# A decode block on one core: the first half of the output rows moves to partitions 28 to 31, and one store replaces two

## The chip, the core and the metric

The kernel runs on one core of a Trainium2 chip. The core has TensorE (PE; its loads of stationary operands are shown apart, as PEld), VectorE (DVE), ScalarE (ACT), GpSimd (POOL) and SyncE (SP), and 16 DMA engines that SP's and ACT's queues feed. The metric is the device time in microseconds (us) of one execution; the median of several runs is compared.

## The reference

One token for each of two sequences (B = 2, D = 448) goes through a normalization, an attention over the last W = 2048 positions of a cache of 8192, and a gate:

```python
xn = layernorm(x)
q = (xn @ wq)                       # 16 heads of 256; 8 KV heads
p = softmax(q . k[:, :, -2048:] * 256 ** -0.5)
s = (p @ v[:, :, -2048:]) @ wo      # back to 448
g = silu(relu(xn @ w1) @ w2)        # 448 -> 1792 -> 448
return x + s * g                    # (2, 1, 448), bfloat16
```

All inputs are bfloat16. The kernel reads 44 MB and writes 1792 bytes.

## The kernel before

The work is split into NU = 4 units: a unit is one sequence and four KV heads, with a K block and a V block of 4 MB each. `_Prog` collects the operations of each engine in a list; each engine runs its list in order, and a list entry names the operations that it waits for (its `deps`), which become waits on semaphores. `pr.dma(SP, ...)` puts a transfer in SP's list, `pr.dma(ACTE, ...)` in ACT's. Nearly all transfers are in SP's list, in this order: wq, w1, w2, the four K blocks, the V blocks (each into its K block's place, once the scores of that unit are done), then wo in five pieces (`WO_PARTS`: 20, 4, 5, 2 and 1 of 32 slices). The lists of PE and DVE are cut at marks into blocks with branches between them (`emit_pe`, `emit_dve`), which bring their code in ahead of time; the order of the work stays as written.

The order of the stages: normalization and clearing of the banks; q = xn @ wq; the gate (`do_H`, `do_F`); for each unit the transposes of K on DVE (L361), the scores (`do_S`), the maximum and the exponential (`do_max`), the transposed weights (`do_et`); then `do_spread` and `do_pt`, the products with V (`do_PV`, `do_out`) and the turning of the result into `at2`, 32 slices of 2 columns each (`do_turn_out`). The matmul instructions all carry the line of the helper `mm`, L313.

The output is kept as four groups of 112 columns (NCOL), numbered c = 2k + h. Group c of sequence b lies in partition 32h + 2b + k: the two groups with h = 0 in partitions 0 to 3, those with h = 1 in partitions 32 to 35. ROWS = 36 partitions are worked on together, those between without use. A row gets to its partition by the stationary operand of the matmul that makes it: two columns of data stand among zero columns in a row of PADW = 5, and a window of 4 columns that starts one column earlier or later (`1 - k : 5 - k`) moves the data to row 2b or 2b + 1. This is done in four places:

- `m_xc` brings x into this layout (stationary `xpad`); ACT copies it to `x_c`, in two copies (L334), POOL has cleared `x_c` before (L251).
- the end of `do_F` does it for the gate (`fpad`, L480), where ACT and DVE then make `g_sb`.
- the tail: `do_turn_out` has filled `at2`. The first 24 slices of wo are multiplied with 2-column stationaries into `wbk` in four column groups of the array (L538), DVE copies `wbk` to `wc` (L541), and four matmuls with `fpad` (float32; each is two records, so 8) bring the sum into `fbk` in the layout above (L547).
- the last 8 slices of wo are multiplied with windows of `at2` straight into the same rows of `fbk` (L553): 8 slices by 4 groups, 32 matmuls, which wait for the third, fourth and fifth piece of wo.

Then DVE multiplies `fbk` with the gate (L559), adds `x_c` (L561) and the two halves leave by two stores, one issued by SP and one by ACT (L563); SP waits for both (L564):

```python
d_o = [pr.dma(eng, half(out, h), out_sb[32 * h:32 * h + 4, :], [v_o]) for h, eng in ((0, SP), (1, ACTE))]
pr.op(SP, None, d_o)
```

Of the kernel before, what the change touches and what calls it, by code (L numbers as in the profile page):

```python
# [5 lines left out]
BF = mybir.dt.bfloat16  # L6
F32 = mybir.dt.float32
ACT = mybir.ActivationFunctionType
ALU = mybir.AluOpType
AX = mybir.AxisListType  # L10

PE, DVE, ACTE, SP, POOL = "pe", "dve", "act", "sp", "pool"
# [121 lines left out]
def bass_recurrent_scan__sliding_block_cached__dense_activation_relu__decode_kernel(  # L134
# [11 lines left out]
    B, Sq, D = A_x.shape  # L146
# [14 lines left out]
    NCOL = D // 4  # L161
    ROWS = 36
    QC = 448
    XW = 160
    PADW = 5
    WO_PARTS = [20, 4, 5, 2, 1]
    WO_TILED = 24

    es = contextlib.ExitStack()
    with es:  # L170
        pr = _Prog(nc, es)

        def named(name, shape, dt):
            return es.enter_context(nc.sbuf_tensor(name, shape, dt))
# [4 lines left out]
        def view(t, off, dims, n=128, p0=0):  # L179
            width = t.shape[1]  # L180
            return bass.AP(t, p0 * width + off, [[width, n]] + dims)
# [6 lines left out]
        wqo = named("wqo", [128, 32 * D], BF)  # L188
# [3 lines left out]
        ident = named("ident", [128, 128], BF)  # L192
# [6 lines left out]
        f8 = named("f8", [128, 8], F32)  # L199
        asel = named("asel", [128, 72], BF)  # L200
        x_sb = named("x_sb", [128, D], BF)
        x_c = named("x_c", [128, NCOL], BF)
# [10 lines left out]
        h_sb = named("h_sb", [128, 448], BF)  # L213
        zc = named("zc", [128, D], F32)
        wc = named("wc", [128, D], F32)
        fpad = named("fpad", [128, PADW], F32)
        xpad = named("xpad", [128, PADW], BF)
        ea = named("ea", [128, NCOL], F32)
        g_sb = named("g_sb", [128, NCOL], F32)
        tmp = named("tmp", [128, NCOL], F32)  # L220
        out_sb = named("out_sb", [128, NCOL], BF)
# [8 lines left out]
        rs = named("rs", [128, 2 * NU], F32)  # L230
        pt = [named(f"pt{i}", [128, 512], BF) for i in range(NU)]
        o_odd = named("o_odd", [128, DH], F32)
        at2 = named("at2", [128, 32 * PADW], BF)

        sbk = [psum(f"sbk{i}", [128, 512], F32) for i in range(2)]
        obk = psum("obk", [128, 512], F32)
        spk = psum("spk", [128, 512], F32)
        mbk = psum("mbk", [128, 512], F32)
        qbk = psum("qbk", [128, 512], F32)
        wbk = psum("wbk", [128, 512], F32)  # L240
        fbk = psum("fbk", [128, 512], F32)

        def half(t, h):
            return t.rearrange("b s (k h n) -> h (b s k) n", h=2, n=NCOL)[h]

        def kv_src(u, cache):
            b, hg = divmod(u, 2)
            return cache[b, 4 * hg:4 * hg + 4, SK - W:SK, :].rearrange("g (p t) d -> p g (t d)", t=NT)

        d_x = pr.dma(ACTE, x_sb[0:B, :], A_x[:, 0, :])  # L250
        p_xc = pr.op(POOL, lambda e: e.memset(x_c[:, :], 0.0))  # L251
        wq_src = A_wq.rearrange("r (hf c) -> (r hf) c", hf=2).rearrange("(p s) c -> p (s c)", s=SLOTS)
        w1_src = B_w1.rearrange("r (hf c) -> (r hf) c", hf=2).rearrange("(p s) c -> p (s c)", s=SLOTS)
        w2_src = B_w2.rearrange("(p j) n -> p (j n)", j=14)
# [3 lines left out]
        st = {}  # L258
# [3 lines left out]
        for u in range(NU):  # L262
# [4 lines left out]
            out=ident[:, :], in_=ident[:, :], compare_op=ALU.not_equal, fill=1.0,  # L267
            base=0, pattern=[[-1, 128]], channel_multiplier=1), [i0])
        p_z = [pr.op(POOL, lambda e, t=t: e.memset(t[:, :], 0.0))
               for t in (fpad, xpad, asel, rm, bt, qstat, at2)][-1]  # L270
# [4 lines left out]
            out=sd[0:B, 0:1], in0=st2[0:B, 1:2], scalar1=EPS, scalar2=None, op0=ALU.add), [v_ag])  # L275
# [5 lines left out]
        def z(t):  # L281
            return a_z[t.name]
# [10 lines left out]
        v_pm = pr.op(DVE, red(pmask[:, :], view(ident, 0, [[1, 4], [4, 32]])))  # L293
        v_g8 = pr.op(DVE, red(view(g8, 0, [[2, 4], [1, 2]]), view(ident, 0, [[32, 4], [1, 2], [2, 4]])))
        v_f8 = pr.op(DVE, red(f8[:, :], view(ident, 0, [[1, 8], [8, 16]])))
        v_fp = pr.op(DVE, lambda e: e.tensor_copy(view(fpad, 1, [[2, B]]), f8[:, 0:B]), [v_f8, p_z])
        v_xp = pr.op(DVE, lambda e: e.tensor_copy(view(xpad, 1, [[2, B]], n=B), ident[0:B, 0:B]), [p_z])
        v_h2 = pr.op(DVE, red(half2[:, :], view(ident, 0, [[8, 2], [16, 8], [1, 8]]), AX.XY))
        v_gs = pr.op(DVE, lambda e: e.tensor_copy(
            view(gsum, 0, [[8, 16], [1, 8]]), view(g8, 0, [[0, 16], [1, 8]])), [v_g8])  # L300
# [11 lines left out]
        def mm(out_ap, lhsT, rhs, start, stop=False, **kw):  # L312
            return lambda e: e.matmul(out_ap, lhsT=lhsT, rhs=rhs, start=start, stop=stop,  # L313
                                      skip_group_check=True, **kw)
# [13 lines left out]
        deps = [v_xp, d_x, z(sbk[1])]  # L328
        for c in range(4):
            k, h = divmod(c, 2)  # L330
            m_xc = pr.op(PE, mm(sbk[1][32 * h:32 * h + 4, 0:NCOL], xpad[0:B, 1 - k:5 - k],
                                x_sb[0:B, NCOL * c:NCOL * c + NCOL], k == 0, k == 1, tile_position=(0, 32 * h)), deps)
            deps = []
        d_xc = [pr.op(ACTE, lambda e, h=h: e.activation(  # L334
            x_c[32 * h:32 * h + 4, :], sbk[1][32 * h:32 * h + 4, 0:NCOL], ACT.Copy), [m_xc, p_xc]) for h in range(2)]

        deps = [d_wq, v_xr, z(qbk)]
        for s in range(SLOTS):
# [24 lines left out]

        def do_S(u):
            b, hg = divmod(u, 2)
            deps = [st["turn", u], st["q"], z(sbk[u % 2]), d_xc[1], st.get(("exp", u - 2))]
            for jp in range(8):
                j, par = divmod(jp, 2)
                for g in range(4):
                    o = pr.op(PE, mm(sbk[u % 2][32 * g:32 * g + 8, :],  # L370
                                     view(qstat, jp * 16 + 4 * g + 2 * hg + b, [[128, 8]]),
                                     view(kv[u], 64 * j + 2 * g + par, [[DH, NT], [8, 8]]),
                                     jp == 0, jp == 7, tile_position=(0, 32 * g)), deps)
                    deps = []
            last_S[u] = o
# [70 lines left out]
        def do_turn_out(hg):  # L446
            deps = [st["osb", 2 + hg], v_as, st["mbk"]]
            lo = 64 * hg
            for dq in range(8):
                o = pr.op(PE, mm(mbk[lo:lo + 64, 288:352], asel[:, 7 - dq:71 - dq],  # L450
                                 view(o_sb, hg * 2 * DH + 32 * dq, [[DH, B], [1, 32]]),
                                 dq == 0, dq == 7, tile_position=(0, lo)), deps)
                deps = []
            st["at"] = st["mbk"] = pr.op(DVE, lambda e: e.tensor_copy(
                view(at2, 1, [[2, B], [PADW, 32]], n=64, p0=lo), view(mbk, 288, [[32, B], [1, 32]], n=64, p0=lo)), [o, p_z])

        def do_H():
            deps = [st["w1"], v_xh, v_q]
# [10 lines left out]
        def do_F():  # L469
            deps = [st["w2"], st["h"], z(fbk)]  # L470
            for j in range(14):
                i = j % 4
                o = pr.op(PE, mm(fbk[32 * i:32 * i + B, 0:D], h_sb[:, 32 * j:32 * j + 2], w2_sb[:, j * D:j * D + D],
                                 j < 4, j >= 10, tile_position=(0, 32 * i)), deps)
                deps = []
            v = pr.op(DVE, lambda e: e.tensor_copy(zc[:, :], fbk[:, 0:D]), [o])
            deps = [v, v_fp, st["mbk"]]
            for c in range(4):
                k, h = divmod(c, 2)
                o = pr.op(PE, mm(mbk[32 * h:32 * h + 4, 0:NCOL], fpad[:, 1 - k:5 - k],  # L480
                                 zc[:, NCOL * c:NCOL * c + NCOL], k == 0, k == 1, tile_position=(0, 32 * h)), deps)
                deps = []
            a_e = pr.op(ACTE, lambda e: e.activation(ea[0:ROWS, :], mbk[0:ROWS, 0:NCOL], ACT.Exp, scale=-1.0), [o])
            v = pr.op(DVE, lambda e: e.tensor_scalar(
                out=ea[0:ROWS, :], in0=ea[0:ROWS, :], scalar1=1.0, scalar2=None, op0=ALU.add), [a_e])
            v = pr.op(DVE, lambda e: e.reciprocal(tmp[0:ROWS, :], ea[0:ROWS, :]), [v])
            st["g"] = st["mbk"] = pr.op(DVE, lambda e: e.tensor_tensor(
                out=g_sb[0:ROWS, :], in0=mbk[0:ROWS, 0:NCOL], in1=tmp[0:ROWS, :], op=ALU.mult), [v])
# [46 lines left out]
        deps = [st["at"], z(wbk)]  # L535
        for j in range(WO_TILED):
            i = j % 4
            o = pr.op(PE, mm(wbk[32 * i:32 * i + B, 0:D], view(at2, PADW * j + 1, [[2, B]]), wqo[:, j * D:j * D + D],  # L538
                             j < 4, j >= WO_TILED - 4, tile_position=(0, 32 * i)), deps + [landed.get(j)])
            deps = []  # L540
        v_wc = pr.op(DVE, lambda e: e.tensor_copy(wc[:, :], wbk[:, 0:D]), [o])  # L541
# [2 lines left out]

        for c in range(4):
            k, h = divmod(c, 2)
            pr.op(PE, mm(fbk[32 * h:32 * h + 4, 0:NCOL], fpad[:, 1 - k:5 - k],  # L547
                         wc[:, NCOL * c:NCOL * c + NCOL], k == 0, tile_position=(0, 32 * h)), deps + [v_wc])
        for j in range(WO_TILED, 32):
            for c in range(4):  # L550
                k, h = divmod(c, 2)
                lo = j * D + c * NCOL
                m_o = pr.op(PE, mm(fbk[32 * h:32 * h + 4, 0:NCOL], at2[:, PADW * j + 1 - k:PADW * j + 5 - k],  # L553
                                   wqo[:, lo:lo + NCOL], False, j == 31,
                                   tile_position=(0, 32 * h)), deps + [landed.get(j)])
                deps = []
# [2 lines left out]
        v_t = pr.op(DVE, lambda e: e.tensor_tensor(  # L559
            out=tmp[0:ROWS, :], in0=fbk[0:ROWS, 0:NCOL], in1=g_sb[0:ROWS, :], op=ALU.mult), [m_o, st["g"]])  # L560
        v_o = pr.op(DVE, lambda e: e.tensor_tensor(  # L561
            out=out_sb[0:ROWS, :], in0=tmp[0:ROWS, :], in1=x_c[0:ROWS, :], op=ALU.add), [v_t] + d_xc)
        d_o = [pr.dma(eng, half(out, h), out_sb[32 * h:32 * h + 4, :], [v_o]) for h, eng in ((0, SP), (1, ACTE))]  # L563
        pr.op(SP, None, d_o)  # L564
        pr.op(PE, None, [v_o])

        pr.run()
# [28 lines left out]
```

## Time and profile before

| | |
|---|---|
| median of 3 runs | 110.27 us (109.98 to 110.44) |
| profiled execution, its own time | 110.19 us |
| its span, first to last instruction | 108.9 us |
| mean granted TensorE clock | 0.859 |
| PE / DVE / ACT / POOL busy | 60.8 / 62.3 / 9.5 / 2.2 us |
| DMA | 44.16 MB, mean 406 GB/s |

The span is that of one profiled execution; the time of an execution is longer by what lies around it (1.3 us here). The profile is a page of the whole span and views that a trace answers. In the page's slices each digit is the busy share of 1/40 of the span in tenths. In a group's row, `out<-in (partitions x elements, type) xcount` is followed by the busy time, the mean ns of one and the idle time of the engine before it with what ended it. In the chain of waits each line is start, length, engine, what was worked on. Rows of an issue (`DMA_DIRECT2D`, engine with a q) last as long as the engine's sequencer was busy with issuing, not as long as the transfer. Matmul ends are modelled.

### The profile page before, as it was taken

The page shows a single profiled execution, that of the slowest core. Times are in us where ns is not written, and L with a number is a line of the kernel's source. Part 1 is how long each engine was busy: PE and PEld are TensorE (multiplying, and loading weights), DVE is VectorE, ACT ScalarE, POOL GpSimd, SP SyncE. Part 2 cuts the span into 40 slices and gives each one's busy share as a digit, 9 for nine tenths or more (in the row PEclk, how much of TensorE's full clock was granted, in tenths as well). Part 3 has the DMA queues.
Part 4 walks back from the last instruction along what each step waited for, and adds up shares of the span by engine and source line. Part 5 has one row for each costly group of instructions (what it writes and reads, how often), then busy time and mean ns, then how long its engine had stood idle before and what let it go on. Part 6 is the DMA issues. An engine that isn't in the chain of part 4 may idle for free.

```text
span 108.9 us, 1103 instructions
## 1 busy us (share of the span) xinstructions
PE 60.8 (56%) x459; PEld 16.4 (15%) x459; DVE 62.3 (57%) x87; ACT 9.5 (9%) x20; POOL 2.2 (2%) x14
## 2 busy tenths in 40 slices
PE   0002195943000069929961996299538966769672
PEld 0001023411000001101100220012023222303131
DVE  1933007344299979999999999940448332203021
ACT  4735000000000000002000200020020000000000
POOL 7000000000000000000000000000000000000000
PEclk9999999999655557995998599769965699999999
DMA  6899999999999999999999999999999899999960
GB/s 165 337 438 405 413 433 493 411 433 470 433 397 433 470 433 397 433 470 433 397 409 494 433 397 409 494 433 397 409 494 433 373 409 439 427 417 428 385 245 1
DMA packets 2471, 44.16 MB, mean 406 GB/s; under 512 B 290, under 2 KB 548, under 8 KB 804
## 3 DMA queue, kind: packets, MB, share of 16 engines
q1 hardware_dynamic: 2456, 44.11, 95.1%
q8 instruction: 3, 0.05, 0.2%
q10 hardware_dynamic: 12, 0.00, 0.0%
HBM read 44.11 MB, written 0.00 MB: 405 GB/s over the span
## 4 chain that ended last, share of the span: by engine, by line
DMA 55%; DVE 29%; PE 9%; SPq 4%; issue 1%
DMA kv<-in_A_k_cache_dram 33%; DVE kv L361 24%; DMA wqo<-in_A_wo_dram 22%; PE sbk L313 7%; SPq L39 4%; PE fbk L313 1%; PE wbk L313 1%; DVE q_x L390 1%; DVE rm L378 1%; DVE wc L541 1%; DVE rm_t L380 0%; DVE bias L384 0%; DVE bt L381 0%; DVE tmp L559 0%; DVE out_sb L561 0%
## 5 line engine op out<-in xcount | busy, mean ns | idle before, releaser
L313 PE MATMUL sbk<-kv,qstat 128*8 128x512 bf16 x128 | 30.0, 1091 | 21.3 <-DVE kv L361 21.3
L361 DVE STREAM_TRANSPOSE kv<-kv 128x2048 f32<-128x2048 f32 x16 | 35.6, 2275 | 3.0 <-DMA kv<-in_A_k_cache_dram 3.0
L313 PEld LDWEIGHTS sbk<-kv,qstat 128*8 128x8 bf16 x128 | 4.9, 107 | 44.9 <-DVE kv L361 27.2
L313 PE MATMUL obk<-kv,pt 128*16 128x512 bf16 x128 | 9.5, 441 | 2.5 <-DVE xg L442 1.2
L439 DVE TENSOR_SCALAR o_odd<-obk,rs 128x256 f32<-128x256 f32 x4 | 1.9, 484 | 11.1 <-PE obk L313 11.1
L385 ACT ACTIVATE e_sb<-sbk,bias 128x512 bf16<-128x512 f32 x4 | 2.7, 687 | 50.2 <-DVE bias L384 50.2
L313 PE MATMUL sbk<-kv,f 128*8 128x512 f32 x14 | 7.0, 620 | 0.0
L378 DVE TENSOR_REDUCE rm<-sbk 128x1 f32<-128x512 f32 x4 | 2.6, 662 | 4.8 <-PE sbk L313 4.8
L313 PE MATMUL qbk<-wqo,xr 128*4 128x512 bf16 x28 | 3.2, 626 | 3.9 <-DMA wqo<-in_A_wq_dram 3.9
L313 PE MATMUL mbk<-ident,xg 2*128 2x2 bf16 x7 | 0.3, 160 | 8.6 <-issue 8.6
L313 PEld LDWEIGHTS obk<-kv,pt 128*16 128x16 bf16 x128 | 3.2, 97 | 8.7 <-issue 5.0
L313 PE MATMUL qbk<-w_sb,xg 128*128 128x448 bf16 x14 | 4.4, 495 | 0.0
L344 DVE TENSOR_SCALAR q_x<-qbk 128x512 bf16<-128x512 f32 x1 | 0.7, 691 | 6.3 <-PE qbk L313 6.3
L390 DVE STREAM_TRANSPOSE q_x<-e_sb 128x512 bf16<-128x512 bf16 x4 | 2.8, 691 | 1.7 <-ACT e_sb L385 1.7
L407 DVE TENSOR_TENSOR pt<-spk,pmask 128x512 bf16<-128x512 f32 x4 | 2.6, 684 | 0.7 <-PE spk L313 0.7
L541 DVE COPY wc<-wbk 128x448 f32<-128x448 f32 x1 | 0.6, 624 | 3.8 <-PE wbk L313 3.8
L313 PE MATMUL spk<-q_x,perm 128*32 128x128 bf16 x16 | 0.6, 294 | 3.1 <-DVE q_x L390 3.1
L355 DVE CAST qstat<-mbk 32x256 bf16<-32x256 f32 x4 | 1.7, 421 | 0.7 <-PE mbk L313 0.7
L464 DVE TENSOR_SCALAR h_n<-qbk 128x448 bf16<-128x448 f32 x1 | 0.6, 623 | 2.6 <-PE qbk L313 2.6
L313 PEld LDWEIGHTS qbk<-w_sb,xg 128*128 128x128 bf16 x14 | 1.7, 130 | 2.3 <-issue 2.0
L442 DVE SCALAR_TENSOR_TENSOR xg<-obk,rs,o_odd 128x256 bf16<-128x256 f32 x4 | 1.9, 484 | 0.1
L272 DVE BATCH_NORM_STATS2 st<-x_sb 2x6 f32<-2x448 bf16 x1 | 0.6, 616 | 2.3 <-DMA x_sb<-in_A_x_dram 2.3
(79 smaller groups left out, 36.0 us busy)
## 6 DMA issues: line engine op xcount, KB each, us to landing
kv<-in_A_k_cache_dram SPq DMA_DIRECT2D x4, 4096.0 KB, 40.4
kv<-in_A_v_cache_dram SPq DMA_DIRECT2D x3, 4096.0 KB, 22.2
kv<-in_A_v_cache_dram SPq DMA_DIRECT2D x2, 2048.0 KB, 17.6
wqo<-in_A_wq_dram SPq DMA_DIRECT2D x1, 3584.0 KB, 12.3
w_sb<-in_B_w_dram SPq DMA_DIRECT2D x2, 1568.0 KB, 17.2
wqo<-in_A_wo_dram SPq DMA_DIRECT2D x1, 2240.0 KB, 24.4
wqo<-in_A_wo_dram SPq DMA_DIRECT2D x1, 560.0 KB, 25.8
wqo<-in_A_wo_dram SPq DMA_DIRECT2D x1, 448.0 KB, 24.8
```

The costliest lines, as they stand in the source:

```text
L39: o = _Op(eng, lambda e: e.dma_start(dst, src), [d for d in deps if d is not None], True)
L313: return lambda e: e.matmul(out_ap, lhsT=lhsT, rhs=rhs, start=start, stop=stop, skip_group_check=True, **kw)
L344: v_q = pr.op(DVE, lambda e: e.tensor_scalar(out=view(q_x, 0, [[256, 8], [128, 2], [1, 32]]), in0=view(qbk, 0, [[64, 8], [1, 2], [2, 32]]) ...
L355: st["q"] = st["mbk"] = pr.op(DVE, lambda e, Q=Q: e.tensor_copy(qstat[32 * Q:32 * Q + 32, 256 * Q:256 * Q + 256], mbk[32 * Q:32 * Q + 32, ...
L361: st["turn", u] = pr.op(DVE, lambda e, n=n: e.transpose(kf[:, 2048 * n:2048 * n + 2048], kf[:, 2048 * n:2048 * n + 2048]), [d_k[u]])
L378: v = pr.op(DVE, lambda e: e.tensor_reduce(out=rm[:, 0:1], in_=sbk[u % 2][:, :], axis=AX.X, op=ALU.max), [last_S[u], p_z, st.get(("rmt", u ...
L385: st["exp", u] = pr.op(ACTE, lambda e: e.activation(e_sb[:, :], sbk[u % 2][:, :], ACT.Exp, bias=bias[:, 0:1], accum_out=ssum[:, u:u + 1]), ...
L390: st["et", u] = pr.op(DVE, lambda e: e.transpose(q_x[:, 512 * u:512 * u + 512], e_sb[:, :]), [st["exp", u], m_qt])
L407: st["pt", u] = pr.op(DVE, lambda e: e.tensor_tensor(out=view(pt[u], 0, [[8, 64], [2, 4], [1, 2]]), in0=view(spk, 128 * u, [[2, 64], [0, 4 ...
L439: v = pr.op(DVE, lambda e: e.tensor_scalar(out=o_odd[:, :], in0=obk[:, DH:2 * DH], scalar1=rs[:, 2 * u + 1:2 * u + 2], scalar2=None, op0=A ...
L442: st["osb", u] = pr.op(DVE, lambda e: e.scalar_tensor_tensor(out=o_sb[:, lo:lo + DH], in0=obk[:, 0:DH], scalar=rs[:, 2 * u:2 * u + 1], in1 ...
L541: v_wc = pr.op(DVE, lambda e: e.tensor_copy(wc[:, :], wbk[:, 0:D]), [o])
```

## The change

The rows with h = 0 move from partitions 0 to 3 to partitions 28 to 31, so that the output stands in 28 to 35 without a gap. A matmul's output can start at partition 0 or 32 here, so the h = 0 matmuls now write 32 rows, 0 to 31, with a window of 32 columns as stationary, whose last 4 columns are the old window; `fpad`, `xpad` and `at2` get LEAD = 28 columns ahead of them. In rows 0 to 27 stands what the columns ahead give (zeros, or data of slices before), which nobody reads. The moving operands, the number of matmuls and their order stay. `x_c` is made by one ACT copy of 36 rows and isn't cleared any more. The output leaves by one store of SP, 8 rows of 112, for which the output in DRAM is addressed as [h, (b, k), n]; ACT stores nothing.

```diff
+    LEAD = 28
-        fpad = named("fpad", [128, PADW], F32)
-        xpad = named("xpad", [128, PADW], BF)
+        fpad = named("fpad", [128, LEAD + PADW], F32)
+        xpad = named("xpad", [128, LEAD + PADW], BF)
-        at2 = named("at2", [128, 32 * PADW], BF)
+        at2 = named("at2", [128, LEAD + 32 * PADW], BF)
-        def half(t, h):
-            return t.rearrange("b s (k h n) -> h (b s k) n", h=2, n=NCOL)[h]
+        def window(t, off, k, h):
+            lo = LEAD + off + 1 - k
+            return t[:, lo:lo + 4] if h else t[:, lo - LEAD:lo + 4]
+
+        def rows_of(t, h, lo=0):
+            return t[32 * h:32 * h + 4, lo:lo + NCOL] if h else t[0:32, lo:lo + NCOL]
-        p_xc = pr.op(POOL, lambda e: e.memset(x_c[:, :], 0.0))
...
-            m_xc = pr.op(PE, mm(sbk[1][32 * h:32 * h + 4, 0:NCOL], xpad[0:B, 1 - k:5 - k],
+            m_xc = pr.op(PE, mm(rows_of(sbk[1], h), window(xpad, 0, k, h)[0:B],
-        d_xc = [pr.op(ACTE, lambda e, h=h: e.activation(
-            x_c[32 * h:32 * h + 4, :], sbk[1][32 * h:32 * h + 4, 0:NCOL], ACT.Copy), [m_xc, p_xc]) for h in range(2)]
+        d_xc = pr.op(ACTE, lambda e: e.activation(x_c[0:ROWS, :], sbk[1][0:ROWS, 0:NCOL], ACT.Copy), [m_xc])
...
-                o = pr.op(PE, mm(mbk[32 * h:32 * h + 4, 0:NCOL], fpad[:, 1 - k:5 - k],
+                o = pr.op(PE, mm(rows_of(mbk, h), window(fpad, 0, k, h),
...
-            pr.op(PE, mm(fbk[32 * h:32 * h + 4, 0:NCOL], fpad[:, 1 - k:5 - k],
+            pr.op(PE, mm(rows_of(fbk, h), window(fpad, 0, k, h),
...
-                m_o = pr.op(PE, mm(fbk[32 * h:32 * h + 4, 0:NCOL], at2[:, PADW * j + 1 - k:PADW * j + 5 - k],
+                m_o = pr.op(PE, mm(rows_of(fbk, h), window(at2, PADW * j, k, h),
...
-        d_o = [pr.dma(eng, half(out, h), out_sb[32 * h:32 * h + 4, :], [v_o]) for h, eng in ((0, SP), (1, ACTE))]
-        pr.op(SP, None, d_o)
+        d_o = pr.dma(SP, out.rearrange("b s (k h n) -> h (b s k) n", h=2, n=NCOL), out_sb[LEAD:ROWS, :], [v_o])
+        pr.op(SP, None, [d_o])
```

The columns at which `fpad`, `xpad` and `at2` are filled, and the 2-column stationaries of `at2` (L538), move by LEAD; `do_S` and the last DVE operation wait for the one copy in place of the two.

More of the change, by code (lines that the diff above doesn't have):

```diff
@@ L295, in bass_recurrent_scan__sliding_block_cached__dense_activation_relu__decode_kernel @@
         v_f8 = pr.op(DVE, red(f8[:, :], view(ident, 0, [[1, 8], [8, 16]])))
-        v_fp = pr.op(DVE, lambda e: e.tensor_copy(view(fpad, 1, [[2, B]]), f8[:, 0:B]), [v_f8, p_z])
-        v_xp = pr.op(DVE, lambda e: e.tensor_copy(view(xpad, 1, [[2, B]], n=B), ident[0:B, 0:B]), [p_z])
+        v_fp = pr.op(DVE, lambda e: e.tensor_copy(view(fpad, LEAD + 1, [[2, B]]), f8[:, 0:B]), [v_f8, p_z])
+        v_xp = pr.op(DVE, lambda e: e.tensor_copy(view(xpad, LEAD + 1, [[2, B]], n=B), ident[0:B, 0:B]), [p_z])
         v_h2 = pr.op(DVE, red(half2[:, :], view(ident, 0, [[8, 2], [16, 8], [1, 8]]), AX.XY))
@@ L365, in do_S @@
             b, hg = divmod(u, 2)
-            deps = [st["turn", u], st["q"], z(sbk[u % 2]), d_xc[1], st.get(("exp", u - 2))]
+            deps = [st["turn", u], st["q"], z(sbk[u % 2]), d_xc, st.get(("exp", u - 2))]
             for jp in range(8):
@@ L454, in do_turn_out @@
             st["at"] = st["mbk"] = pr.op(DVE, lambda e: e.tensor_copy(
-                view(at2, 1, [[2, B], [PADW, 32]], n=64, p0=lo), view(mbk, 288, [[32, B], [1, 32]], n=64, p0=lo)), [o, p_z])
+                view(at2, LEAD + 1, [[2, B], [PADW, 32]], n=64, p0=lo), view(mbk, 288, [[32, B], [1, 32]], n=64, p0=lo)), [o, p_z])
         def do_H():
@@ L537, in bass_recurrent_scan__sliding_block_cached__dense_activation_relu__decode_kernel @@
             i = j % 4
-            o = pr.op(PE, mm(wbk[32 * i:32 * i + B, 0:D], view(at2, PADW * j + 1, [[2, B]]), wqo[:, j * D:j * D + D],
+            o = pr.op(PE, mm(wbk[32 * i:32 * i + B, 0:D], view(at2, LEAD + PADW * j + 1, [[2, B]]), wqo[:, j * D:j * D + D],
                              j < 4, j >= WO_TILED - 4, tile_position=(0, 32 * i)), deps + [landed.get(j)])
@@ L561, in bass_recurrent_scan__sliding_block_cached__dense_activation_relu__decode_kernel @@
         v_o = pr.op(DVE, lambda e: e.tensor_tensor(
-            out=out_sb[0:ROWS, :], in0=tmp[0:ROWS, :], in1=x_c[0:ROWS, :], op=ALU.add), [v_t] + d_xc)
-        d_o = [pr.dma(eng, half(out, h), out_sb[32 * h:32 * h + 4, :], [v_o]) for h, eng in ((0, SP), (1, ACTE))]
-        pr.op(SP, None, d_o)
+            out=out_sb[0:ROWS, :], in0=tmp[0:ROWS, :], in1=x_c[0:ROWS, :], op=ALU.add), [v_t, d_xc])
+        d_o = pr.dma(SP, out.rearrange("b s (k h n) -> h (b s k) n", h=2, n=NCOL), out_sb[LEAD:ROWS, :], [v_o])
+        pr.op(SP, None, [d_o])
         pr.op(PE, None, [v_o])
```

## The prediction

> **What bounds the kernel now.** First the page: span, the slices and the chain.
>
> ```profile
> span 108.9 us, 1103 instructions
> ...
> DMA  6899999999999999999999999999999899999960
> ...
> DMA 55%; DVE 29%; PE 9%; SPq 4%; issue 1%
> ```
>
> The DMA engines are full from the second slice (2.7 us) to slice 38, so everything ahead of the last weight rows is paced by transfers, and a step there that does not delay a transfer costs nothing. What can move the time is the tail behind the last transfer. The chain of waits, in order of time (start, length, what), gives that tail:
>
> ```profile
> 78.86 24.37 DMA wqo<-in_A_wo_dram
> ...
> 103.36 1.38 PE wbk L313 x24
> ...
> 104.77 0.63 DVE wc L541
> ...
> 105.45 1.42 PE fbk L313 x40
> ...
> 106.90 0.28 DVE tmp L559
> ...
> 107.20 0.27 DVE out_sb L561
> ```
>
> The chain ends at 107.20 + 0.27 = 107.47 us, but the span is 108.9: the last 1.4 us are the stores. The timeline of the end shows the stages that the change touches (the last two lines are the two stores as SP and ACT issue them), and SP's waits show what follows:
>
> ```profile
> 105.45 0.29 PEld L313 LDWEIGHTS fbk<-wc,fpad 128*4 128x4 f32 x8 [1.00 <-DVE wc L541]
> ...
> 105.78 0.90 PEld L313 LDWEIGHTS fbk<-wqo,at 128*4 128x4 bf16 x32
> 105.84 1.02 PE L313 MATMUL fbk<-wqo,at 128*4 128x112 bf16 x32
> ...
> 107.49 0.35 SPq L39 DMA_DIRECT2D out_dram<-out_sb  x1
> 107.50 0.28 ACTq L39 DMA_DIRECT2D out_dram<-out_sb  x1
> ```
>
> ```profile
> SPq L69 <- DMA out_dram<-out_sb: 1.0, 1, 1.0
> ```
>
> SP issues until 107.84 and then waits 1.0 us for landings: the span ends there. That wait covers both stores. The semaphore instructions by engine (count, ns least/median/most, first and last start in us) tell which part of it is the second store:
>
> ```profile
> L69 PEldq EVENT_SEMAPHORE  x12: 51/51/5912, 8.5 to 107.5; - x12
> L69 DVEq EVENT_SEMAPHORE  x2: 21/21/21, 3.5 to 82.4; - x2
> ...
> L69 SPq EVENT_SEMAPHORE  x1: 183/183/183, 108.7 to 108.7; - x1
> ```
>
> SP's instruction waits for two semaphores, starts at 108.7 and lasts 183 ns, where one whose condition is already met costs 21 ns on DVE and 51 on TensorE. My reading: it starts when the first store has landed and ends when the second has, so the landings lie about 183 - 50 = 0.13 us or more apart. Which is second? The packets of the DMA queues, for three stretches of the end (107.40 to 108.90 in 40 slices of 37.5 ns; then 108.240 to 108.273; then 108.34 to 108.37), where q1 is SP's queue and q10 ACT's:
>
> ```profile
> GB/s 0 0 0 0 0 0 0 0 0 0 0 0 0 0 0 0 0 0 0 0 0 0 6 24 12 6 0 0 0 0 0 0 0 0 0 0 0 0 0 0
> ...
> q1 hardware_dynamic: 8, 0.00, 0.5%
> q10 hardware_dynamic: 8, 0.00, 0.5%
> ```
>
> ```profile
> q10 hardware_dynamic: 3, 0.00, 8.5%
> ```
>
> ```profile
> q1 hardware_dynamic: 2, 0.00, 5.2%
> ```
>
> All bytes move between 107.4 + 22 x 0.0375 = 108.23 and 108.38: 0.74 us after the issue began, and 0.5 us before the end. ACT's packets go first and SP's last. So the end is: issue to first packet 0.74, packets 0.13, then 0.5 of waiting for the last completion, of which some 0.13 to 0.18 is the second store's.
>
> **The change, part by part.**
>
> Head. The clearing of x_c on POOL goes, three other clears grow by a few columns, and two ACT copies of x_c become one. These rows (POOL, then PE, then ACT) show the cover:
>
> ```profile
> 0.73 0.19 POOL L251 MEMSET x_c<- 128x112 bf16 x1 [0.29 <-POOLq L581]
> ...
> 9.27 0.53 ACT L334 ACTIVATE x_c<-sbk 4x112 bf16<-4x112 f32 x2 [2.91 <-PE sbk L313]
> ...
> 13.11 3.16 PE L313 MATMUL qbk<-wqo,xr 128*4 128x512 bf16 x28 [3.88 <-DMA wqo<-in_A_wq_dram]
> ```
>
> TensorE idles 3.88 us until the first weights land at 13.1, and x_c is read at 107.20 and its bank needed only in the K stage. Worth 0; without the cover it would be -0.19 on POOL and about -0.27 on ACT, gains both.
>
> The gate stage (do_F). Its four matmuls get wide stationaries too. They end long before the K cache is there: the transposes of the K blocks start after an idle time set by a transfer.
>
> ```profile
> 25.64 0.55 PE L313 MATMUL mbk<-zc,fpad 128*4 128x112 f32 x8 [0.72 <-DVE zc L476]
> ...
> 30.18 4.50 DVE L361 STREAM_TRANSPOSE kv<-kv 128x2048 f32<-128x2048 f32 x2 [2.26 <-DMA kv<-in_A_k_cache_dram]
> ```
>
> The 2.26 us of idle DVE hide any growth of a 0.55 us group. Worth 0; uncovered, at most the price per load below times 4.
>
> The tail on TensorE. Half of the 40 loads for fbk (h = 0) go from 4 to 32 columns: 4 of the f32 records, 16 of the bf16. Mean ns of a load by width (mean after the comma):
>
> ```profile
> L313 PEld LDWEIGHTS fbk<-wqo,at 128*4 128x4 bf16 x32 | 0.8, 84 | 0.1
> ...
> L313 PEld LDWEIGHTS mbk<-xg,asel 128*64 128x64 bf16 x16 | 0.7, 111 | 2.8 <-DVE xg L442 2.8
> ...
> L313 PEld LDWEIGHTS mbk<-ssum,gsum 128*128 128x128 f32 x2 | 0.5, 310 | 0.2 <-issue 0.2
> ...
> L313 PEld LDWEIGHTS fbk<-wc,fpad 128*4 128x4 f32 x8 | 0.3, 86 | 1.0 <-DVE wc L541 1.0
> ```
>
> Per column, bf16: (111 - 84)/60 = 0.45 ns; f32: (310 - 86)/124 = 1.8 ns. So 28 more columns cost 13 ns in bf16 and 51 ns in f32. If nothing hides a load: 16 x 13 + 4 x 51 = 0.41 us, the upper end. But loads run ahead under the matmul before them: eight loads of 64 columns with their matmuls took 0.44 us altogether,
>
> ```profile
> 100.14 0.44 PE L313 MATMUL mbk<-xg,asel 128*64 128x64 bf16 x8 [0.27 <-DVE xg L442]
> ```
>
> under 55 ns for each pair, although one load lasts 111. The lower end is therefore 0. Only a load with no matmul before it is exposed. There is also a cover, since the tail is still fed by transfers: the loads of the last two pieces of wo, and where the bytes end (106.2 to 106.6 in slices of 10 ns):
>
> ```profile
> 106.34 0.19 PEld L313 LDWEIGHTS fbk<-wqo,at 128*4 128x4 bf16 x8
> ```
>
> ```profile
> 106.59 0.09 PEld L313 LDWEIGHTS fbk<-wqo,at 128*4 128x4 bf16 x4
> ```
>
> ```profile
> GB/s 0 90 0 0 0 0 0 0 0 0 0 0 0 0 0 0 0 0 0 0 0 0 0 0 0 0 0 0 0 0 0 0 0 0 0 0 0 0 0 0
> ```
>
> The last 4 loads start at 106.59, 0.06 us after the group of 8 stopped loading, and 0.37 us after the last bytes moved: I read this as a wait for that last piece's landing. The f32 growth falls ahead of this wait. What stays is the first load behind it: +0.01 to +0.02 us. I take +0.02, range 0 to +0.41.
> The Trainium skill, "TensorE: Matmul & The Clock Gate", section "LDWEIGHTS (loading the stationary operand)", prices a load at its columns divided by 1.2 in ns: 28 columns would be 23 ns, and 20 such loads +0.47 us by it if they stood in a row. The trace here shows 13 per bf16 load, and pairs closer together than a load is long.
>
> The stores. ACT's store goes (issue 0.28 us, off the path beside SP's), with its wait and its completion; SP's store has 8 rows of 224 B, and on the DRAM side its address pattern has one more level. SP has nothing queued behind it except the final wait, so a longer issue moves only the landing. Issue times in ns (least/median/most):
>
> ```profile
> L39 SPq DMA_DIRECT2D kv<-in_A_v_cache_dram x5: 535/535/604, 46.7 to 78.2; - x5
> L39 SPq DMA_DIRECT2D wqo<-in_A_wo_dram x5: 432/432/592, 78.9 to 80.9; - x5
> L39 SPq DMA_DIRECT2D kv<-in_A_k_cache_dram x4: 594/611/1786, 2.1 to 5.3; - x4
> ...
> L39 SPq DMA_DIRECT2D out_dram<-out_sb x1: 347/347/347, 107.5 to 107.5; - x1
> ```
>
> V loads have the extra level (the head), wo loads do not: 535 against 432, so +0.10 us as the upper end of a plain store; 0 as the lower. V also has more rows to describe, so I take +0.03. Packets: 8 data packets as now, up to +0.1 if they run on fewer engines, I take +0.02. Completion: the second landing goes, -0.13 to -0.18; 0 if SP's store lands late by itself rather than for standing behind ACT's. I take -0.15, and -0.01 for one wait in place of two.
>
> Sum: 0.02 + 0.03 + 0.02 - 0.15 - 0.01 = -0.09 us. The profiled execution took 110.19 us (its span and 1.3 around it, which I leave): 110.10. It stands 0.08 under the median of the runs, 110.27, and against that the forecast is 110.18. Bounds of the parts: best 0 + 0 + 0 - 0.18 - 0.05 = -0.23; worst 0.41 + 0.10 + 0.10 + 0 = +0.61.
>
> **The rivals.**
>
> *No gain: the eight rows take what two stores took.* For it: rows of both halves alternate in 224 B pieces in DRAM, which stays so, and 0.13 us may be a write's own time. Against it: ACT's store, which has the same kind of rows, landed first. Place: SP's last wait. Price: 0 saved, +0.03 to +0.20 for issue and packets, so 110.30 to 110.47; I put it at 110.38.
> A rule bears on this: the Trainium skill, "DMA: Bandwidth & Descriptors", section "Why a DMA increments its semaphore by 16 and not by 1", has a DMA use the largest number of engines that divides the slowest dimension of both sides. The 8 packets a queue seen here fit 4 rows and 4 completions; by that rule dimensions 8 and 2 give 2 engines with 4 rows each, the +0.1 of the packets.
>
> *Loads are exposed.* If a 32-column load cannot run under a matmul on the neighbouring columns, the tail takes the whole 0.41 us: 110.27 + 0.41 - 0.11 = 110.57. Against it: the 55 ns pairs. It is what the LDWEIGHTS rule above would make of it, without the cover.
>
> *Slower: one long issue.* The first K load's issue, of the same three-level kind, lasted 1786 ns where its like took 594 to 611. If the one store, issued after 26 us of rest on SP, is issued as slowly, the end moves by 1.44 - 0.16: 111.55. It turns the sign by over 0.5% from an issue of 347 + 550 + 160 = about 1060 ns. Against it: the first V load came 41 us after the last K load, none of the five took over 604, and the first K load stood behind three others.
>
> *Faster by over 0.5%.* That takes 0.55 us out of 1.4 from the issue to the end, and the rows show 0.18 of a second store. Only if the 0.5 us from last packet to end were mostly two queues in each other's way: 110.27 - 0.55, 109.7.
>
> **How the numbers follow.** A difference within 0.5%, 0.55 us, can't be told from no change here. Forecast 0.60 (110.05 to 110.27, with the scatter of runs 109.95 to 110.35); no gain 0.22; exposed loads 0.06; long issue 0.07; faster 0.05. Of the exposed loads a third lies beyond 0.5%: slower 0.09, faster 0.05, same 0.86. The range 109.9 to 110.5 holds the first two cases with the scatter of a median (0.2 either way): about 8 in 10.
>
> **What would show it.** Right: SP's last semaphore instruction, for one store now, short (under 60 ns) and the span's end some 1.25 us behind the issue; SP's issue row 350 to 400 ns; loads of fbk with 32 columns near 97 ns, the fbk step within 0.03 of 1.42 us; 10 to 16 packets at the end, all on q1. Wrong: an issue row over 0.5 us; a last wait as long as 1.0 us; gaps between the last matmuls.

## The result, and the profile after

| | before | changed |
|---|---|---|
| median of 21 runs each | 110.25 us | 110.77 us |
| profiled execution, its time | 110.19 us | 110.83 us |
| its span | 108.9 us | 109.4 us |

The changed kernel is slower: ratio 1.0044, 95% interval 1.0030 to 1.0059, that is +0.49 us (0.33 to 0.65). The forecast was 110.18 with a range up to 110.5.

The timeline of the changed kernel's tail, rows as before:

```profile
104.83 0.62 DVE L544 COPY wc<-wbk 128x448 f32<-128x448 f32 x1 [3.81 <-PE wbk L317]
...
107.27 0.27 DVE L564 TENSOR_TENSOR out_sb<-tmp,x_c 36x112 bf16<-36x112 f32 x1
107.56 0.77 SPq L39 DMA_DIRECT2D out_dram<-out_sb  x1
```

```profile
L39 SPq DMA_DIRECT2D out_dram<-out_sb x1: 773/773/773, 107.6 to 107.6; - x1
```

From the start of the copy to `wc` to the end of the last addition it is 107.27 + 0.27 - 104.83 = 2.71 us, where the kernel before has 107.20 + 0.27 - 104.77 = 2.70. The wide stationaries cost 0.01 us. (The copy itself starts 0.06 us later in this execution. Ahead of it TensorE waits for the first weights of wo, 0.97 us in both traces, and the start differs by more than this from execution to execution: it lies between 104.63 and 105.09 us in the kept traces.) What is new is the last line: SP needs 0.77 us to issue the store, in place of 0.35 (in ns, 773 and 347). SP's wait for the landing, its last semaphore instruction, and the packets from 107.5 to 109.4 in slices of 47.5 ns:

```profile
SPq L69 <- DMA out_dram<-out_sb: 1.0, 1, 1.0
```

```profile
L69 SPq EVENT_SEMAPHORE  x1: 17/17/17, 109.4 to 109.4; - x1
```

```profile
GB/s 0 0 0 0 0 0 0 0 0 0 0 0 0 0 0 0 0 0 0 0 0 0 0 0 0 0 0 0 0 0 28 10 0 0 0 0 0 0 0 0
...
q1 hardware_dynamic: 10, 0.00, 0.5%
```

The reader is to see two things. SP's last instruction is short now, 17 ns in place of 183: there is no second landing to wait for. But SP still waits 1.0 us behind its issue row, as before, and the bytes start to move only at 107.5 + 30 x 0.0475 = 108.93, 1.37 us behind the start of the issue.

The stretch from the start of SP's issue to the end of its last instruction, taken from the trace's records in ns:

| stretch | before | changed | difference |
|---|---|---|---|
| start of the issue to SP's first packet | 781 | 1375 | +594 |
| to the last completion packet | 83 | 56 | -27 |
| to the last landing | 489 | 350 | -139 |
| to the end of SP's last instruction | 23 | 34 | +11 |
| sum | 1376 | 1815 | +439 |

0.44 us here and 0.01 on TensorE are the 0.49 us that the runs show, within the interval. Of the 594 ns, 426 are the longer issue row (347 to 773); the other 168 lie between the end of the issue row and SP's first packet (434 ns before, 602 now).

### The profile page after: what moved, and what is told of

The parts are those of the page before. It is cut to its first block, busy times and chain, and to the rows that moved or that the text cites. A ratio compares the mean times of both kernels' runs of the same rounds, so it can differ in the third digit from the quotient of the medians.

```text
span 109.4 us, 1099 instructions
## 1 busy us (share of the span) xinstructions
PE 59.4 (54%) x459; PEld 16.3 (15%) x459; DVE 62.3 (57%) x87; ACT 9.3 (8%) x19; POOL 2.1 (2%) x13
## 4 chain that ended last, share of the span: by engine, by line
DMA 55%; DVE 29%; PE 9%; SPq 4%; issue 1%
DMA kv<-in_A_k_cache_dram 33%; DVE kv L364 24%; DMA wqo<-in_A_wo_dram 22%; PE sbk L317 7%; SPq L39 4%; PE fbk L317 1%; PE wbk L317 1%; DVE q_x L393 1%; DVE rm L381 1%; DVE wc L544 1%; DVE rm_t L383 0%; DVE bias L387 0%; DVE bt L384 0%; DVE tmp L562 0%; DVE out_sb L564 0%
## 5 line engine op out<-in xcount | busy, mean ns | idle before, releaser
L317 PE MATMUL sbk<-kv,f 128*8 128x512 f32 x14 | 7.6, 660 | 0.0
L317 PEld LDWEIGHTS obk<-kv,pt 128*16 128x16 bf16 x128 | 3.7, 98 | 8.2 <-issue 5.2
L317 PE MATMUL qbk<-w_sb,xg 128*128 128x448 bf16 x14 | 2.8, 352 | 0.0
L317 PE MATMUL wbk<-wqo,at 128*2 128x448 bf16 x24 | 1.4, 351 | 1.0 <-DMA wqo<-in_A_wo_dram 1.0
L317 PEld LDWEIGHTS sbk<-kv,f 128*8 128x8 f32 x14 | 1.3, 96 | 3.1 <-issue 2.6
```

## The experiments

The theories: **A**, the whole loss is in the one store, and in it in the issue; as its cause A1 the second level of the address pattern, A2 the number of engines, A3 the number of rows, and A4, formed after the first four runs, that the two sides of the transfer are cut differently. **B**, the wide stationaries or the moved rows have a part.

**Two stores again, in the wide layout** (two runs, `wide_two_stores` and `wide_two_again`)

```diff
-        d_o = pr.dma(SP, out.rearrange("b s (k h n) -> h (b s k) n", h=2, n=NCOL), out_sb[LEAD:ROWS, :], [v_o])
-        pr.op(SP, None, [d_o])
+        halves = out.rearrange("b s (k h n) -> h (b s k) n", h=2, n=NCOL)
+        d_o = [pr.dma(eng, halves[h], out_sb[LEAD + 4 * h:LEAD + 4 * h + 4, :], [v_o]) for h, eng in ((0, SP), (1, ACTE))]
+        pr.op(SP, None, d_o)
```

> The changed kernel with its wide stationaries and its rows in partitions 28 to 35, but with two stores of four rows again, one issued by SP and one by ACT. Theory A (the loss is all in the one store): as the kernel before, 110.25 us within 0.1; SP's issue row back from 773 ns to about 350, last semaphore instruction of SP about 0.18 us. Rival B (the wide stationaries, or the moved rows, cost a part of it): between 110.35 and 110.7, and the fbk step longer than 1.42 us.

Measured: 110.59 us, ratio to the kernel before 1.0019 (1.0000 to 1.0038). The issue rows and the last wait of this run:

```profile
L39 SPq DMA_DIRECT2D out_dram<-out_sb x1: 347/347/347, 107.4 to 107.4; - x1
L39 ACTq DMA_DIRECT2D out_dram<-out_sb x1: 278/278/278, 107.4 to 107.4; - x1
```

```profile
L69 SPq EVENT_SEMAPHORE  x1: 182/182/182, 108.5 to 108.5; - x1
```

The issue rows and the last wait are those of the kernel before within 1 ns, and the end comes 1356 ns behind the start of the issue (1376 before), yet the median stood between the theories. So the pair was measured again, together with the changed kernel unaltered (`changed_again`):

> The two stores in the wide layout once more, for its interval, since 1.0019 (1.0000 to 1.0038) stood between the theories while its trace has the tail of the kernel before. Theory A: ratio to the kernel before 1.0002, 110.3 us, and the changed kernel about 0.45 us over it. Rival B: 1.002 or more again.

> The changed kernel as it is, beside the run with two stores in the wide layout. Theory A: the difference between the two is all of the loss, about 0.45 us, ratio to the kernel before 1.004. Rival B: the difference is 0.25 us, and the wide layout has the rest.

Measured: two stores 110.27 us, ratio 0.9992 (0.9977 to 1.0008); the changed kernel 110.68 us, ratio 1.0041 (1.0019 to 1.0063); the kernel before 110.31 us. The difference of 0.41 us is the store's. B falls: the layout costs nothing that these runs can tell. The 1.0019 I read as scatter, since the two intervals overlap (1.0000 to 1.0008) and the first trace shows no longer tail; the stretch from the copy to `wc` to the last addition is 2.70 to 2.72 us in the traces with wide stationaries and a whole last addition, 2.70 in those without.

**One store of eight rows on one level** (`one_store_flat`)

```diff
-        d_o = pr.dma(SP, out.rearrange("b s (k h n) -> h (b s k) n", h=2, n=NCOL), out_sb[LEAD:ROWS, :], [v_o])
+        d_o = pr.dma(SP, out.rearrange("b s (c n) -> (b s c) n", n=NCOL), out_sb[LEAD:ROWS, :], [v_o])
```

> The changed kernel, but its one store writes the eight rows to DRAM in the order of the partitions, so that the DRAM side has one level of eight rows instead of two levels of 2 and 4 (the output's groups stand in the wrong order by that). Theory A1 (the second level of the address pattern costs the 0.43 us of issue): SP's issue row about 350 to 400 ns, 110.1 us. Theory A2 (two engines in place of four or eight cost it): the same here, since eight rows on one level would go to eight engines: 18 packets at the end (16 if the records pair otherwise). Theory A3 (eight rows in place of four cost it): issue row still near 770 ns, 110.75 us.

Measured: 110.18 us beside 110.33 of the kernel before, ratio 0.9988 (0.9968 to 1.0008). Issue row, last wait, packets:

```profile
L39 SPq DMA_DIRECT2D out_dram<-out_sb x1: 367/367/367, 107.8 to 107.8; - x1
```

```profile
L69 SPq EVENT_SEMAPHORE  x1: 17/17/17, 109.0 to 109.0; - x1
```

```profile
q1 hardware_dynamic: 16, 0.00, 0.3%
```

Eight rows are issued in 367 ns: A3 falls. The 16 packets are 8 rows and 8 completions. From the start of the issue to the end it is 1254 ns, 122 under the kernel before. This is what the prediction had expected of the change. It is no kernel to keep, since the output is in another order, and no run stored eight rows on one level in the reference's order.

**One store with levels of 4 and 2** (`one_store_4x2`)

```diff
-        d_o = pr.dma(SP, out.rearrange("b s (k h n) -> h (b s k) n", h=2, n=NCOL), out_sb[LEAD:ROWS, :], [v_o])
+        d_o = pr.dma(SP, out.rearrange("b s (c n) -> c (b s) n", n=NCOL), out_sb[LEAD:ROWS, :], [v_o])
```

> The changed kernel, but the one store's DRAM side has levels of 4 and 2 rows in place of 2 and 4 (again in another order of the output's groups). Theory A1 (the second level costs the issue time): row near 770 ns, 110.75 us. Theory A2 (the count of engines costs it: by the rule 4 here, 12 packets at the end, where the changed kernel has 2 and 10): row near 350 ns, 110.1 us.

Measured: 111.03 us, the median of five runs, ratio 1.0066 (1.0035 to 1.0097). Issue row and packets:

```profile
L39 SPq DMA_DIRECT2D out_dram<-out_sb x1: 786/786/786, 107.5 to 107.5; - x1
```

```profile
q1 hardware_dynamic: 12, 0.00, 0.2%
```

12 packets are 8 rows and 4 completions, where the changed kernel has 2. Read as one completion for each engine these are four engines, and the issue is as slow as with two. A2 falls. The end comes 1825 ns behind the start of the issue, 10 later than in the changed kernel.

**The kernel before with SP's store alone** (`before_half`)

```diff
-        d_o = [pr.dma(eng, half(out, h), out_sb[32 * h:32 * h + 4, :], [v_o]) for h, eng in ((0, SP), (1, ACTE))]
-        pr.op(SP, None, d_o)
+        d_o = pr.dma(SP, half(out, 0), out_sb[0:4, :], [v_o])
+        pr.op(SP, None, [d_o])
```

> The kernel before without ACT's store: only SP's four rows are written, the other half of the output is left out. The prediction's term of the second landing, -0.13 to -0.18 us: SP's last semaphore instruction short, the span's end 1.20 to 1.25 us behind the start of SP's issue in place of 1.38, 110.1 us. If SP's store lands late by itself: no change, 110.25 us.

Measured: 110.15 us, ratio 0.9989 (0.9971 to 1.0006), too small a difference for the runs. In the trace the end is 1207 ns behind the start of the issue, 169 under the kernel before:

```profile
L39 SPq DMA_DIRECT2D out_dram<-out_sb x1: 348/348/348, 107.5 to 107.5; - x1
```

```profile
L69 SPq EVENT_SEMAPHORE  x1: 17/17/17, 108.6 to 108.6; - x1
```

SP's store of the same four rows, issued in the same time, lands earlier when ACT's isn't beside it: the term of the second landing is as large as predicted.

**The store twice** (`store_twice`)

```diff
-        d_o = pr.dma(SP, out.rearrange("b s (k h n) -> h (b s k) n", h=2, n=NCOL), out_sb[LEAD:ROWS, :], [v_o])
-        pr.op(SP, None, [d_o])
+        d_o = []
+        for _ in range(2):
+            d_o = [pr.dma(SP, out.rearrange("b s (k h n) -> h (b s k) n", h=2, n=NCOL), out_sb[LEAD:ROWS, :], [v_o] + d_o)]
+        pr.op(SP, None, d_o)
```

> The changed kernel with its store made twice, the second when the first has landed. Theory A1a (the pattern with two levels costs SP its 0.43 us each time): both issue rows near 775 ns, the end 1.8 us later than with one store. Rival A1b (only the first use of such a pattern after a long rest is slow): first row near 775 ns, second near 370 to 450.

Measured: 112.28 us in one run beside 110.58 of the kernel before. Both issue rows are in this group (least, median, most):

```profile
L39 SPq DMA_DIRECT2D out_dram<-out_sb x2: 679/726/774, 107.4 to 109.2; - x2
```

The first use costs 95 ns more than the second; the second is still nearly twice a plain store's. So a first use is worth at most those 95 ns of the surplus. The end comes 1.73 us later behind the first issue than in the changed kernel, as A1a had it. This run and the next three were made once each, so that their times tell little; it is their issue rows that decide.

**Two levels on both sides** (`matched_levels`)

```diff
-        d_o = pr.dma(SP, out.rearrange("b s (k h n) -> h (b s k) n", h=2, n=NCOL), out_sb[LEAD:ROWS, :], [v_o])
+        rows = e_sb[0:4, 0:240].rearrange("p (g m) -> p g m", g=2)[:, :, 0:NCOL]
+        d_o = pr.dma(SP, out.rearrange("b s (c n) -> c (b s) n", n=NCOL), rows, [v_o, st["exp", NU - 1]])
```

> The changed kernel, but the one store takes its 8 rows from 4 partitions with two pieces each (of another tile, so that the output's values are not the reference's), and writes them to DRAM with levels of 4 and 2: both sides have two levels of the same sizes, where the changed kernel has 8 on the SBUF side and 2 by 4 on the DRAM side. Theory A1 (a second level in the pattern costs the issue time): row near 775 ns. Rival A4 (the two sides being cut differently costs it): row near 350 to 450 ns.

Measured: 110.35 us in one run beside 110.58. Issue row:

```profile
L39 SPq DMA_DIRECT2D out_dram<-e_sb x1: 339/339/339, 107.8 to 107.8; - x1
```

The DRAM side is that of the run with levels of 4 and 2, with 786 ns; only the SBUF side changed, from 8 rows to 4 by 2. A1 falls as it was put: a second level costs nothing if both sides have it. A4 holds for these stores.

A4 is no general price, though, as a row of the prediction shows. The V loads are cut differently on their two sides as well: `kv_src` has 32 rows by 4 heads (`"g (p t) d -> p g (t d)"`), the SBUF side 128 partitions. Their issue took 535 ns beside 432 for the wo loads, which have 128 on both sides, so 0.10 us more, not the 0.41 of the changed kernel's store (773 against 367). Nor do the stores separate "the same levels" from "the same first level": where the issue was quick the first levels are equal (2, 4 or 8 on both sides), where it was slow they are 8 against 2 or 4.

**Two rows** (`two_rows`) **and the store from ACT** (`act_store`)

```diff
-        d_o = pr.dma(SP, out.rearrange("b s (k h n) -> h (b s k) n", h=2, n=NCOL), out_sb[LEAD:ROWS, :], [v_o])
+        d_o = pr.dma(SP, out.rearrange("b s (c n) -> (b s c) n", n=NCOL)[0:2], out_sb[LEAD:LEAD + 2, :], [v_o])
```

> The changed kernel, but the one store writes two rows on one level (the other six are left out), which gives two engines as the changed store has them: 4 packets at the end. Theory A1: issue row near 350 ns, the count of engines is nothing. Theory A2 (few engines are slow to issue for): near 775 ns.

```diff
-        d_o = pr.dma(SP, out.rearrange("b s (k h n) -> h (b s k) n", h=2, n=NCOL), out_sb[LEAD:ROWS, :], [v_o])
+        d_o = pr.dma(ACTE, out.rearrange("b s (k h n) -> h (b s k) n", h=2, n=NCOL), out_sb[LEAD:ROWS, :], [v_o])
```

> The changed kernel, but its one store of two levels is issued by ACT. ACT issued the four rows of one level in 277 ns where SP took 347. Theory A1: slow on ACT too, near 0.7 us, the span's end 1.7 to 1.8 us behind the last addition. Rival A5 (it is SP's state after its rest): near 300 ns and an end 1.25 us behind it.

Measured, one run each: 109.99 and 110.65 us beside 110.58. Issue rows, of the two rows and of ACT's store, and the packets of the two rows:

```profile
L39 SPq DMA_DIRECT2D out_dram<-out_sb x1: 331/331/331, 107.4 to 107.4; - x1
```

```profile
L39 ACTq DMA_DIRECT2D out_dram<-out_sb x1: 708/708/708, 107.5 to 107.5; - x1
```

```profile
q1 hardware_dynamic: 4, 0.00, 0.1%
```

Two rows left 4 packets, so 2 completions as in the changed kernel, and were issued in 331 ns: A2 falls a second time. ACT needs 708 ns where its four rows on one level took 277: a surplus of 0.43 us over four plain rows on this engine too, as on SP, so it isn't SP's state.

**A store of one level without the wide stationaries** (`pool_half`, `dve_two`). The output is brought into the order of DRAM by the last addition:

```diff
-            out=out_sb[0:ROWS, :], in0=tmp[0:ROWS, :], in1=x_c[0:ROWS, :], op=ALU.add), [v_t] + d_xc)
-        d_o = [pr.dma(eng, half(out, h), out_sb[32 * h:32 * h + 4, :], [v_o]) for h, eng in ((0, SP), (1, ACTE))]
-        pr.op(SP, None, d_o)
+            out=out_sb[0:4, 0:NCOL], in0=tmp[0:4, :], in1=x_c[0:4, :], op=ALU.add), [v_t] + d_xc)
+        p_o = pr.op(POOL, lambda e: e.tensor_tensor(
+            out=out_sb[0:4, NCOL:2 * NCOL], in0=tmp[32:36, :], in1=x_c[32:36, :], op=ALU.add), [v_t] + d_xc)
+        d_o = pr.dma(SP, out.rearrange("b s (k m) -> (b s k) m", m=2 * NCOL), out_sb[0:4, :], [v_o, p_o])
+        pr.op(SP, None, [d_o])
```

> The kernel before (4-column stationaries), but the last addition is cut in two, and the half with h = 1, which POOL makes beside DVE, is written from partitions 32 to 35 into partitions 0 to 3, columns 112 to 223. The output then stands in 4 partitions of 224 columns, in the order of DRAM, and one SP store of one level with 4 rows of 448 B takes it. By theory A1 and the term of the second landing: issue row near 350 ns, the end 1.20 to 1.25 us behind the start of the issue in place of 1.38. If POOL's half takes no longer than DVE's 0.27 us: 110.1 us, 0.13 under the kernel before; it is a loss if POOL takes over 0.4 us.

In `dve_two` the line with `POOL` has `DVE`.

> As the run with the half on POOL, but DVE makes both halves, one after the other: +0.12 to 0.2 us for the second addition, -0.15 for the landing: 110.2 to 110.3 us, no difference to the kernel before that can be measured. The wide stationaries' rival would see no change here, since there are none.

Measured: 110.41 us, ratio 1.0012 (0.9990 to 1.0033), and 110.52 us, ratio 1.0015 (0.9996 to 1.0034); the kernel before 110.27. The timeline of the first:

```profile
107.25 0.26 DVE L561 TENSOR_TENSOR out_sb<-tmp,x_c 4x112 bf16<-4x112 f32 x1
107.30 0.47 POOL L563 TENSOR_TENSOR out_sb<-tmp,x_c 4x112 bf16<-4x112 f32 x1 [104.35 <-DVE tmp L559]
107.86 0.35 SPq L39 DMA_DIRECT2D out_dram<-out_sb  x1
```

The store does what was hoped (1224 and 1227 ns from issue to end), but POOL's half ends 0.26 us behind DVE's, and on DVE the second half is 0.3 us more. The gain of 0.15 is spent ahead of the store. No run beat the kernel before by more than its interval. Of those with an interval that wrote the whole output, the lowest were the one store on one level (0.9988, in another order) and the second measurement of the two stores in the wide layout (0.9992).

## Why the prediction was wrong

The direction and the size were wrong: -0.09 us was forecast, +0.49 measured, and the median of 110.77 lies 0.27 us beyond the range. That the time still stayed within 0.5% of the kernel before, which had the largest chance, is luck: the forecast was a small gain, and the interval of what came reaches 1.0059.

- *The head and the gate stage, 0.* Right as far as the trace shows: in both traces TensorE waits 0.97 us for the first weights of wo, so what lies ahead of them set nothing.
- *The tail on TensorE, +0.02.* Right: 0.01. Loads by width in the changed kernel:

```profile
L317 PEld LDWEIGHTS fbk<-wqo,at 128*32 128x32 bf16 x16 | 0.9, 97 | 0.0
L317 PEld LDWEIGHTS fbk<-wqo,at 128*4 128x4 bf16 x16 | 0.8, 84 | 0.0
...
L317 PEld LDWEIGHTS fbk<-wc,fpad 128*32 128x32 f32 x4 | 0.3, 109 | 1.0 <-DVE wc L544 1.0
...
L317 PEld LDWEIGHTS fbk<-wc,fpad 128*4 128x4 f32 x4 | 0.3, 86 | 0.0
```

  A bf16 load of 32 columns takes 97 ns, 13 over one of 4, as worked out. In f32 it is 23, not 51. The 51 came from a row at another clock: the 310 ns of the 128-column f32 load were taken at 81.2 us, where the granted clock (third number from the end of the two stretches' rows) was 0.50, and the tail runs at 1.00:

```profile
81.23 0.50 PEld L313 LDWEIGHTS mbk<-ssum,gsum 128*128 128x128 f32 x2 [0.21 <-issue]
```

```profile
81.20:81.90 0.70, 0.62 (x6) 0.50 (x2) 0.55 (x1) 0.00 (x0) 0.00 (x0) 0.50 1.52 655
105.40:106.95 1.55, 1.40 (x40) 1.11 (x40) 0.05 (x1) 0.00 (x0) 0.00 (x0) 1.00 0.13 36
```

  Half of 51 is near the 23 measured, though no run changed the clock alone. As an estimate from the Trainium skill's section "LDWEIGHTS (loading the stationary operand)" of "TensorE: Matmul & The Clock Gate", 28 columns are 23 ns, which agrees with the f32 row here and not with the bf16 one. Neither came to the end, since the loads run under matmuls; the rival of exposed loads (+0.41) did not happen.
- *The second landing, -0.15, and one wait for two, -0.01.* The first is right: the last landing follows 139 ns sooner on its completion packet, and the run without ACT's store showed 169 in all. The second gained nothing: from the last landing to the end it is 34 ns, where it was 23.
- *Packets, +0.02.* No row stood behind this term, and it was too high by 0.05: they took 27 ns less. There were 10, 8 rows and 2 completions, which agrees with the rule of the Trainium skill ("DMA: Bandwidth & Descriptors", "Why a DMA increments its semaphore by 16 and not by 1") on the number of engines, as do the 12, 16 and 4 packets of the other patterns. Two completions instead of four cost nothing: the end came 1815 ns behind the issue with two and 1825 with four (`one_store_4x2`).
- *The issue, +0.03.* This is the step that failed. It was bounded by the V loads, "535 against 432, so +0.10 us as the upper end", as the nearest row with an extra level. Measured: +0.43 for the issue, and another 0.17 until the first packet. For the second part the prediction had no term: it took a longer issue to move the packets by as much and no more. In the runs SP's first packet came 0.42 to 0.44 us behind the end of its issue row where the two sides are cut alike, and 0.60 to 0.63 where they are not. The term was mis-sized because a price was carried over from loads of 2 and 4 MB to a store of 1.8 KB. A level by itself isn't what costs: with two levels on both sides the issue took 339 ns. What costs in this store is that one side has 8 rows on one level and the other has 2 by 4 (773) or 4 by 2 (786). The V loads have such a difference too and pay 0.10 us for it.

The rival "one long issue" named the right place, SP's issue row, but not the size: its price was that of the first K load, and by its own point of decision (about 1060 ns) 773 would not have been over 0.5%. An issue row between the V loads' and that was in none of the cases. Two of the signs of being wrong that the prediction named itself came: "an issue row over 0.5 us" and "a last wait as long as 1.0 us".

What stays open: why a pattern cut differently on its two sides costs this, and why it costs four times as much in the short store as in the V loads, which differ from it in direction, length of rows and number of rows. No run here looks into the issue. It also isn't tried whether the surplus grows with the rows; all the stores that were cut differently had eight.

## What to carry to other kernels

When two small stores are made one, compare the shapes of both sides: a store whose SBUF side and DRAM side have the same levels was issued by SP here in 0.33 to 0.37 us, one whose sides were cut differently in 0.68 to 0.79, and at the end of a kernel all of that is time. Two stores side by side on two queues aren't free either: SP's landed 0.17 us earlier when ACT's wasn't beside it. And a bound that is read from a row of another kind of transfer (long rows, deep in a stream) is no bound for the last short one; the price of a new pattern should be left open upward.

## What the runs showed that was not expected

- The surplus of a store cut differently: 0.41 us of issue on SP against eight rows on one level (773 and 367), 0.43 against four (347), 0.43 on ACT against four (708 and 277), and 0.1 less when it is used a second time at once (679). A load cut differently paid 0.10 (535 and 432).
- SP's store of four rows is completed later beside one of ACT: alone it ended 1207 ns behind its issue, beside ACT's 1376. Whether ACT's is delayed as well wasn't tried.
- One store of eight rows on one level ends sooner than two of four rows: 1254 ns and 1376.
